# QK-normed attention and a token/channel mixer on one core: attention one element ahead, weights converted in two staggered halves, key norms in the exp's scale, a compact reciprocal

## The chip, the core and the metric

One core of a Trainium2 chip runs the whole program. The metric is the device time of one execution in microseconds. The kernel before takes 1813.64 us (median of 3 runs, 1812.88 to 1815.33).

## The reference

Eight elements, twelve heads, 448 tokens, 64 columns a head. The four mixer weights come in as 64-bit floats, everything else as 32-bit.

```python
def rmsnorm(x, g):
    return x / np.sqrt(np.mean(x * x, axis=-1, keepdims=True) + 1e-06) * g
scores = np.matmul(rmsnorm(q, g_q), rmsnorm(k, g_k).transpose(0, 1, 3, 2)) / np.sqrt(64)
attn = np.exp(scores - max(scores)); attn = attn / (sum(attn) + 1e-09)
x = (attn @ v), heads side by side              # (8, 448, 768)
h = np.maximum(x.transpose(0, 2, 1) @ w_tok1, 0.0) @ w_tok2      # 448 -> 256 -> 448
u = x + h.transpose(0, 2, 1)
return u + np.maximum(u @ w_ch1, 0.0) @ w_ch2                    # 768 -> 1536 -> 768
```

## The kernel before

**Two halves of the work.** Attention goes by pairs of heads: 8 elements x 6 pairs = 48 pairs, two steps each (`att_step`, L334). A step computes the scores of half of the key tokens (`score`, L242: four matmuls into four PSUM buffers of `ps_S`, then four exps on ScalarE into `e`), adds the exps of the key chunks on VectorE (`chunk_sums`, L286), and multiplies the exps of the step before with the values (`av`, L297). Once per pair a matmul with ones spreads the sums over the rows (`denominator`, L312), and VectorE takes the reciprocal (L328) and multiplies the products with it into `uT` (L329). The norms of the next pair (`norm_pair`, L202) are squares on GpSimd (L211), a sum on VectorE (L213), a power of -1/2 on GpSimd (L217) and the scaling of queries and keys on GpSimd (L221). `trans_qk` (L227) transposes them on TensorE into a buffer of `ps_M`, which has two, and copies them out with the gain, the queries on VectorE (L238) and the keys on ScalarE (L240). The mixing of an element (`mlp_items`, L449) transposes `uT` to `x` (L375), mixes tokens (L390, L398), then channels (L413 with `w_ch1`, L425 with `w_ch2`), transposes the result to `y` (L437) and stores it (L444). `x` and `y` share one buffer.

**Weights.** The 64-bit weights are split into 80 chunks of 256 columns: 4 of `w_tok1`, 4 of `w_tok2`, 36 of `w_ch1`, 36 of `w_ch2`. A chunk is loaded raw from ScalarE's queue (L137, buffers `raw`, three) and put together as a 32-bit float by `weight_convert` (L147): two masks (L162, L163), two steps for the exponent on GpSimd (L165, L166), one for the mantissa on ScalarE (L167), and three more on VectorE (L168, L170, L172). Chunk i's load is issued two chunks ahead.

**Order.** TensorE runs in the order in which the program writes its instructions. On the other engines and queues a planner orders the instructions by its own costs, and each engine then runs its list in order, DMA issues included. `merge` (L23) interleaves lists of items by their stated costs. First the 26 steps of elements 0 and 1 and two steps of element 2 are merged with the 44 chunks of `w_tok1`, `w_tok2` and `w_ch1` (L480). Then the mixing of each element b is merged with the attention of element b + 2 (`AHEAD`, L468). Beside the mixing of element 0, up to its last `w_ch1` matmul, lie the 36 chunks of `w_ch2` (L486). The last two elements mix alone. Ahead of all a comparison of the gains chooses between two copies of the body (L524); in this run the one with `shifted` False is taken.

## Time and profile before

| what | value |
|---|---|
| time, median of 3 runs | 1813.64 us |
| time of the profiled execution | 1814.12 us |
| its span, first to last instruction | 1811.9 us |
| mean granted TensorE clock (1 is 2.4 GHz, 0.5 is 1.2 GHz) | 0.941 |
| TensorE busy | 1570.2 us, 87% |
| VectorE busy | 627.2 us, 35% |
| GpSimd busy | 446.8 us, 25% |
| ScalarE busy | 355.1 us, 20% |
| DMA, mean over the span | 36 GB/s |

The shares are means over stages with different limits, so the stages are read apart: windows give the busy time of each engine, the granted clock and the DMA share of a stretch, and the waits of that stretch say what an idle engine was released by. "Idle before" in square brackets is the time that the engine did nothing ahead of an instruction, with what ended it.

### The profile page before, as it was taken

To read this page: it belongs to the slowest core of one execution; us is meant where nothing else is said; L and a number is where in the kernel's file an instruction comes from. 1 tells how busy PE (TensorE), PEld (TensorE's weight loads), DVE (VectorE), ACT (ScalarE), POOL (GpSimd) and SP (SyncE) were. 2 spreads that over 40 slices of the span, in tenths; PEclk is the share of its full clock that TensorE was granted. 3 is DMA by queue.
4 is the path that set the end of the run, shared out by engine and by line. 5 is a ranking of instruction groups with operands and counts; after the bars stand their busy time and mean duration, and the time that the engine had idled before them with its cause. 6 is when DMAs were issued, how large, how long until landed. Compare 5 with 4: busy or idle time off the path is not lost.

```text
span 1811.9 us, 13526 instructions
## 1 busy us (share of the span) xinstructions
PE 1570.2 (87%) x5248; PEld 743.7 (41%) x5248; DVE 627.2 (35%) x957; ACT 355.1 (20%) x713; POOL 446.8 (25%) x408
## 2 busy tenths in 40 slices
PE   4555456789989998999989998999989998998998
PEld 1121123334444444444444444444444444554554
DVE  4666667772224233322233233232332231000000
ACT  2222223232121211221121212221121211001100
POOL 5655555543111212112112212113113100000000
PEclk8776778989999999999999999999999999999999
DMA  3222223320100001000100001000100000000001
GB/s 97 77 82 75 76 67 95 97 73 26 36 31 16 31 16 46 29 18 16 46 31 16 31 16 56 21 16 28 33 31 16 11 1 31 0 0 31 1 0 32
DMA packets 53838, 65.73 MB, mean 36 GB/s; under 512 B 4164, under 2 KB 43844, under 8 KB 53764
## 3 DMA queue, kind: packets, MB, share of 16 engines
q1 hardware_dynamic: 41986, 44.05, 7.8%
q10 hardware_dynamic: 11778, 20.72, 3.7%
q8 instruction: 43, 0.70, 0.2%
q14 instruction: 31, 0.25, 0.0%
HBM read 53.74 MB, written 11.01 MB: 36 GB/s over the span
## 4 chain that ended last, share of the span: by engine, by line
PE 70%; DVE 13%; POOL 10%; DMA 2%; issue 2%; ACT 2%; ACTq 0%; DVEq 0%; POOLq 0%
PE m_ps L425 24%; PE m_ps L413 22%; PE s_ps L251 6%; PE o_ps L305 5%; PE m_ps L390 4%; DVE rd L328 4%; POOL rs L217 4%; PE m_ps L398 3%; DVE es L295 2%; POOL e_t L166 2%; POOL qs L221 2%; POOL e_t L165 2%; DMA out_dram<-y 2%; PE m_ps L375 2%; PE m_ps L233 1%
## 5 line engine op out<-in xcount | busy, mean ns | idle before, releaser
L413 PE MATMUL m_ps<-uT,wc_sb 128*128 128x448 f32 x1152 | 452.0, 547 | 13.3 <-ACT h L417 6.3
L425 PE MATMUL m_ps<-h,wc_sb 128*128 128x448 f32 x1152 | 450.4, 544 | 9.2 <-DVE uT L430 5.8
L413 PEld LDWEIGHTS m_ps<-uT,wc_sb 128*128 128x128 f32 x1152 | 215.9, 191 | 236.5 <-issue 209.6
L211 POOL TENSOR_TENSOR qs<-qk 112x512 f32<-112x512 f32 x96 | 102.4, 1068 | 830.4 <-PE m_ps L233 769.9
L425 PEld LDWEIGHTS m_ps<-h,wc_sb 128*128 128x128 f32 x1152 | 213.4, 190 | 220.3 <-issue 204.0
L256 ACT ACTIVATE e<-s_ps 112x448 f32<-112x448 f32 x384 | 180.9, 546 | 313.5 <-PE s_ps L251 211.1
L251 PE MATMUL s_ps<-qkT 64*112 64x448 f32 x768 | 191.3, 613 | 16.5 <-DVE qkT L238 6.5
L295 DVE TENSOR_TENSOR es<-es,e 112x896 f32<-112x896 f32 x96 | 108.1, 1126 | 213.8 <-ACT e L256 210.3
L233 PE MATMUL m_ps<-ident,qs 112*128 112x112 f32 x384 | 60.8, 287 | 138.2 <-DVE rd L328 105.2
L305 PE MATMUL o_ps<-e,vt 112*64 112x448 f32 x768 | 171.9, 571 | 0.0
L217 POOL TENSOR_TENSOR rs<-ms,mhalf_c 112x16 f32<-112x16 f32 x48 | 154.1, 3210 | 53.6 <-DVE ms L216 53.5
L430 DVE TENSOR_TENSOR uT<-uT,m_ps 128x448 f32<-128x448 f32 x48 | 29.8, 621 | 374.6 <-PE m_ps L425 374.6
L328 DVE RECIPROCAL rd<-m_ps 128x448 f32<-128x448 f32 x48 | 141.6, 2951 | 5.8 <-PE m_ps L319 5.8
L417 ACT ACTIVATE h<-m_ps 128x448 f32<-128x448 f32 x96 | 52.2, 543 | 403.0 <-PE m_ps L413 401.6
L233 PEld LDWEIGHTS m_ps<-ident,qs 112*128 112x128 f32 x384 | 46.3, 154 | 175.1 <-issue 138.6
L291 DVE TENSOR_TENSOR es<-e 112x896 f32<-112x896 f32 x48 | 52.7, 1099 | 187.3 <-ACT e L256 187.3
L251 PEld LDWEIGHTS s_ps<-qkT 64*112 64x112 f32 x768 | 67.8, 188 | 120.0 <-issue 89.6
L221 POOL TENSOR_TENSOR qs<-qk,rs 112x512 f32<-112x512 f32 x96 | 98.4, 1046 | 3.8
L305 PEld LDWEIGHTS o_ps<-e,vt 112*64 112x64 f32 x768 | 53.0, 143 | 111.4 <-issue 111.4
L390 PE MATMUL m_ps<-x,w_sb 112*128 112x384 f32 x256 | 93.7, 524 | 5.9 <-ACT h L393 5.9
L398 PE MATMUL m_ps<-w_sb,h 128*128 128x448 f32 x192 | 80.1, 559 | 13.7 <-DVE rd L328 11.1
L439 ACT COPY y<-m_ps 112x512 f32<-112x512 f32 x48 | 28.1, 586 | 293.1 <-PE m_ps L437 292.8
(40 smaller groups left out, 793.7 us busy)
## 6 DMA issues: line engine op xcount, KB each, us to landing
raw<-in_moe_w_ch_dram ACTq DMA_DIRECT2D x72, 256.0 KB, 2.6
qk<-in_q_dram SPq DMA_DIRECT2D x48, 224.0 KB, 2.7
qk<-in_k_dram SPq DMA_DIRECT2D x48, 224.0 KB, 2.9
vt<-in_v_dram SPq DMA_DIRECT2D x48, 224.0 KB, 3.0
out_dram<-y SPq DMA_DIRECT2D x16, 672.0 KB, 4.3
raw<-in_moe_w_tok_dram ACTq DMA_DIRECT2D x4, 224.0 KB, 5.1
raw<-in_moe_w_tok_dram ACTq DMA_DIRECT2D x2, 256.0 KB, 2.6
raw<-in_moe_w_tok_dram ACTq DMA_DIRECT2D x2, 192.0 KB, 2.3
```

Of the source, the lines that this page charges most:

```text
L217: nc.gpsimd.tensor_tensor(out=rs[0:R], in0=ms[0:R], in1=mhalf_c[0:R].to_broadcast([R, 2 * n]), op=ALU.pow)
L221: nc.gpsimd.tensor_tensor(out=st["qs", p, i][0:R].rearrange("p c h d -> p h c d"), in0=qk[0:R, i].rearrange("p h (c d) -> p h c d", d=D), ...
L233: nc.tensor.transpose(ps[:, c * R:(c + 1) * R], qs[0:R, c].rearrange("p h d -> p (h d)"), ident[0:R, 0:R])
L251: nc.tensor.matmul(out=ps[0:R, 0:S], lhsT=qkT[a * D:(a + 1) * D, 1, kc * R:(kc + 1) * R], rhs=qkT[a * D:(a + 1) * D, 0, :], start=True, st ...
L256: nc.scalar.activation(out=e[0:R, a, i, :], in_=pss[a][0:R, 0:S], func=AF.Exp)
L295: nc.vector.tensor_tensor(out=es[0:R], in0=es[0:R], in1=e[0:R, :, i, :], op=ALU.add)
L305: nc.tensor.matmul(out=o[a * D:(a + 1) * D, 0:S], lhsT=vt[0:R, a, kc * D:(kc + 1) * D], rhs=e[0:R, a, i, :], start=(kc == 0), stop=(kc == ...
L328: nc.vector.reciprocal(out=rd[:], in_=ps[:, 0:S])
L390: nc.tensor.matmul(out=ps[:, 0:HC], lhsT=w1_sb[0:R, c, jc * P:(jc + 1) * P], rhs=st["x"][0:R, c, cs], start=(c == 0), stop=(c == NS - 1))
L398: nc.tensor.matmul(out=ps[:, 0:S], lhsT=st["h1", jc][:, cc * P:(cc + 1) * P], rhs=w2_sb[:, jc].rearrange("p c r -> p (c r)"), start=(jc == ...
L413: nc.tensor.matmul(out=ps[:, 0:S], lhsT=wc1_sb[:, cc, f * P:(f + 1) * P], rhs=st["uT", b][:, cc, :], start=(cc == 0), stop=(cc == NC - 1))
L425: nc.tensor.matmul(out=ps[:, 0:S], lhsT=wc2_sb[:, f, cc * P:(cc + 1) * P], rhs=st["h2"][:, f, :], start=(f == 0), stop=(f == NF - 1))
```

## The change

Attention now runs one element ahead: element 0's attention alone, then the mixing of element b beside the attention of b + 1, and only the last element mixes alone. Before the first mixing 15 chunks of weights are converted; the other 65, and the last half of the chunk before them, are merged with the mixing of element 0 up to its fourth output column. A chunk is converted in two parts: the masks, exponent and mantissa steps of chunk i are written ahead of the last steps of chunk i - 1; the last multiplication goes from VectorE to GpSimd. Raw loads go out from SyncE's queue, the stores of the result from ScalarE's.

Squares are taken on ScalarE, for queries and keys at once, two pairs ahead; loads of queries and keys lie three pairs ahead, with heads side by side already in SBUF. Only the queries are scaled by their norms; those of the keys are the scale of the exp, which is read per row. Both copies of the transposed queries and keys are on ScalarE. The first of the three sums of exps goes to GpSimd. The denominators come half a pair earlier, and their reciprocal is taken in 14 columns: a transpose in blocks of 32 puts one copy of the sums in few columns, and a second transpose spreads the reciprocals over the rows. The first two loads and the first norms stand ahead of the branch.

```diff
-def whole(ctx, tc, shifted, q, k, v, ...):
+def whole(ctx, tc, shifted, pre, q, k, v, ...):
...
-    raw_pool = pool("raw_pool", 3)
-    cv_pool = pool("cv_pool", 2)
-    qk_pool = pool("qk_pool", 2)
+    raw_pool = pool("raw_pool", 4)
+    cv_pool = pool("cv_pool", 3)
     v_pool = pool("v_pool", 2)
-    qs_pool = pool("qs_pool", 2)
-    st_pool = pool("st_pool", 3)
     qkT_pool = pool("qkT_pool", 2)
     e_pool = pool("e_pool", 2)
-    es_pool = pool("es_pool", 2)
-    rd_pool = pool("rd_pool", 1)
-    uT_pool = pool("uT_pool", 3)
+    es_pool = pool("es_pool", 1)
+    rd_pool = pool("rd_pool", 2)
+    uT_pool = pool("uT_pool", 2)
...
+                second.append((P, moe_w_ch1[t * P:(t + 1) * P, o:o + n], wc1_sb[:, t, o:o + n], None))
         for o in range(0, C, WCOLS):
             for f in range(NF):
                 n = min(WCOLS, C - o)
-                second.append((P, moe_w_ch2[f * P:(f + 1) * P, o:o + n], wc2_sb[:, f, o:o + n], None))
-        return first, second
+                third.append((P, moe_w_ch2[f * P:(f + 1) * P, o:o + n], wc2_sb[:, f, o:o + n], None))
+        return first, second, third
...
     def weight_load(i):
...
-            nc.scalar.dma_start(
+            nc.sync.dma_start(
                 out=t[0:rows, 0:n, :].rearrange("p n w -> p (n w)"), in_=src.bitcast(U32))
...
+    def convert_first(i):
+        rows, src, dst, split = chunks[i]
+        n = src.shape[-1]
+        if src.dtype != I64:
+            return
+        hi = st["raw", i][0:rows, 0:n, 1]
+        e_t = cv_pool.tile([P, WCOLS], U32, name="e_t")
+        m_t = cv_pool.tile([P, WCOLS], U32, name="m_t")
+        st["cv", i] = e_t, m_t
+        e, m = e_t[0:rows, 0:n], m_t[0:rows, 0:n]
+        ef, mf = e.bitcast(F32), m.bitcast(F32)
+        nc.vector.tensor_scalar(e, hi, 0x7FF00000, None, ALU.bitwise_and)
+        nc.vector.tensor_scalar(m, hi, 0x000FFFFF, None, ALU.bitwise_and)
+        nc.gpsimd.tensor_scalar(ef, e, 1151.0 * 2**20, 896.0 * 2**20, ALU.min, ALU.max)
+        nc.gpsimd.tensor_scalar(e, ef, -896.0 * 2**20, 8.0, ALU.add, ALU.mult)
+        nc.scalar.activation(out=mf, in_=m, func=AF.Identity, bias=one_c[0:rows, 0:1], scale=2.0**-20)
...
+    def convert_last(i):
...
         nc.vector.scalar_tensor_tensor(
             out=mf, in0=lo, scalar=2.0**-52, in1=mf, op0=ALU.mult, op1=ALU.add)
         nc.vector.scalar_tensor_tensor(
             out=e, in0=hi, scalar=0x80000000, in1=e, op0=ALU.bitwise_and, op1=ALU.bitwise_or)
-        nc.vector.tensor_tensor(out=dst, in0=fold(mf), in1=fold(ef), op=ALU.mult)
+        nc.gpsimd.tensor_tensor(out=dst, in0=fold(mf), in1=fold(ef), op=ALU.mult)
...
             if i + LOADS_AHEAD < len(chunks):
                 weight_load(i + LOADS_AHEAD)
-            weight_convert(i)
+            if i < len(chunks):
+                convert_first(i)
+            if i:
+                convert_last(i - 1)
         return [(1.0, lambda i=i: one(i)) for i in range(lo, hi)]
...
+    def scale(p):
+        n = 2 * NS
+        for i in range(1 + shifted):
+            x = st["qk", p][0:R, i].rearrange("p c h d -> p (c h) d")
+            r = st["rs", p][0:R, i * n:(i + 1) * n]
+            nc.gpsimd.tensor_tensor(
+                out=x, in0=x, in1=r.unsqueeze(2).to_broadcast([R, n, D]), op=ALU.mult)
...
     def trans_qk(p, i):
...
             nc.tensor.transpose(
-                ps[:, c * R:(c + 1) * R],
-                qs[0:R, c].rearrange("p h d -> p (h d)"), ident[0:R, 0:R])
-        dst = st["qkT", p][:, i, :]
-        if i == 0:
-            nc.vector.tensor_scalar(dst, ps[:, 0:S], g_t[:, i:i + 1], None, ALU.mult)
-        else:
-            nc.scalar.mul(dst, ps[:, 0:S], g_t[:, i:i + 1])
+                ps[:, c * R:(c + 1) * R], qk[0:R, i, c].rearrange("p h d -> p (h d)"), ident[0:R, 0:R])
+        nc.scalar.mul(st["qkT", p][:, i, :], ps[:, 0:S], g_t[:, i:i + 1])
...
-                nc.scalar.activation(out=e[0:R, a, i, :], in_=pss[a][0:R, 0:S], func=AF.Exp)
+                r = 2 * NS + kc * 2 + a
+                nc.scalar.activation(
+                    out=e[0:R, a, i, :], in_=pss[a][0:R, 0:S], func=AF.Exp,
+                    scale=st["rs", p][0:R, r:r + 1])
...
-            nc.vector.tensor_tensor(out=es[0:R], in0=e[0:R, :, 0, :], in1=e[0:R, :, 1, :], op=ALU.add)
+            nc.gpsimd.tensor_tensor(out=es[0:R], in0=e[0:R, :, 0, :], in1=e[0:R, :, 1, :], op=ALU.add)
...
+        nb = S // 32
+        dt = rd_pool.tile([P, S], F32, name="dt", tag="rd")
+        if shifted:
+            nc.vector.tensor_scalar(dt[:], ps[:, 0:S], 1e-9, None, ALU.add)
+            src = dt[:]
+        else:
+            src = ps[:, 0:S]
+        nc.vector.transpose(out=dt[:], in_=src)
+        rc = pre.st_pool.tile([P, nb], F32, name="rc")
+        nc.vector.reciprocal(out=rc[:], in_=dt[:].rearrange("p (n c) -> p n c", c=32)[:, :, 0])
         rd = rd_pool.tile([P, S], F32, name="rd", tag="rd")
-        if shifted:
-            nc.vector.tensor_scalar(rd[:], ps[:, 0:S], 1e-9, None, ALU.add)
-            nc.vector.reciprocal(out=rd[:], in_=rd[:])
-        else:
-            nc.vector.reciprocal(out=rd[:], in_=ps[:, 0:S])
+        nc.vector.transpose(
+            out=rd[:].rearrange("p (n c) -> p n c", c=32), in_=rc[:].unsqueeze(2).to_broadcast([P, nb, 32]))
...
-        if g < NG and h == 0 and p + 2 < NP:
-            items.append((0.0, lambda: load_qk(p + 2)))
+        if g < NG and h == 0 and p + 3 < NP:
+            items.append((0.0, lambda: pre.load_qk(p + 3, st)))
...
         def products():
-            if h == 1 and p >= 1:
-                denominator(p - 1)
             if 1 <= g <= NG:
                 av(*divmod(g - 1, 2))
+            if h == 0 and p >= 1:
+                denominator(p - 1)
         def tiled():
             for part in (products, scores) if shifted else (scores, products):
                 part()
-        items.append((3.6 + 0.8 * h, tiled))
-        if g < NG and p + 1 < NP:
-            if h == 0:
-                items.append((0.0, lambda: norm_pair(p + 1)))
-            else:
-                items += [(0.4, lambda i=i: trans_qk(p + 1, i)) for i in range(2)]
+        items.append((4.4 - 0.8 * h, tiled))
+        if g < NG and h == 0 and p + 2 < NP:
+            items.append((0.0, lambda: pre.norm_pair(p + 2, st)))
+            items.append((0.0, lambda: scale(p + 2)))
+        if g < NG and h == 1 and p + 1 < NP:
+            items += [(0.4, lambda i=i: trans_qk(p + 1, i)) for i in range(2)]
...
-            nc.sync.dma_start(
+            nc.scalar.dma_start(
                 out=out[b].rearrange("(p c) n -> p c n", c=NS)[:, :, cs], in_=st["y"][0:R, :, cs])
...
-        early = items
-        late = []
+        early, late = items, []
         for cc in range(NC):
+            if cc == NC - WCOLS // P:
+                early, late = early + late, []
...
-    first, second = weight_chunks()
-    chunks = first + second
-    AHEAD = 2
-    load_qk(0)
+    first, second, third = weight_chunks()
+    chunks = first + second + third
+    AHEAD = 1
+    BEFORE = len(first) + NC + 1
     load_v(0)
-    load_qk(1)
     for i in range(LOADS_AHEAD):
         weight_load(i)
-    norm_pair(0)
+    scale(0)
     trans_qk(0, 0)
     trans_qk(0, 1)
+    pre.load_qk(2, st)
+    pre.norm_pair(1, st)
+    scale(1)
     per = NPAIR * 2
     att_items = lambda lo, hi: [it for g in range(lo, hi) for it in att_step(g)]
-    for _, fn in merge(att_items(0, AHEAD * per + 2), weight_items(0, len(first))):
+    for _, fn in merge(att_items(0, AHEAD * per + 2), weight_items(0, BEFORE)):
         fn()
     for b in range(B):
         early, late = mlp_items(b)
         if b == 0:
-            early = merge(early, weight_items(len(first), len(chunks)))
+            early = merge(early, weight_items(BEFORE, len(chunks) + 1))
...
+class Start:
+    def __init__(self, ctx, tc, q, k):
+        self.qk_pool = pool("qk_pool", 3)
+        self.sq_pool = pool("sq_pool", 1)
+        self.load_qk(0, self.st)
+        self.load_qk(1, self.st)
+        self.mhalf_c = const.tile([P, 1], F32, name="mhalf_c")
+        nc.gpsimd.memset(self.mhalf_c[:], -0.5)
+        self.norm_pair(0, self.st, apart=True)
+        self.ident = const.tile([P, P], F32, name="ident")
+        make_identity(nc, self.ident[:, :])
+        self.one_c = const.tile([P, D], F32, name="one_c")
+        nc.gpsimd.memset(self.one_c[:], 1.0)
+    def heads(self, p):
+        b, j = divmod(p, self.NPAIR)
+        return b, slice(2 * j, 2 * j + 2)
+    def load_qk(self, p, st):
+        b, hs = self.heads(p)
+        st["qk", p] = qk = self.qk_pool.tile([128, 2, self.NS, 2, self.D], F32, name="qk")
+        for i, src in enumerate((self.q, self.k)):
+            for a in range(2):
+                self.nc.sync.dma_start(
+                    out=qk[0:self.R, i, :, a], in_=src[b, hs][a].rearrange("(p c) d -> p c d", c=self.NS))
+    def norm_pair(self, p, st, apart=False):
+        nc, R, D = self.nc, self.R, self.D
+        n = 2 * self.NS
+        qk = st["qk", p]
+        sq = self.sq_pool.tile([128, 2, n, D], F32, name="sq")
+        ms = self.st_pool.tile([128, 2 * n], F32, name="ms")
+        st["rs", p] = rs = self.st_pool.tile([128, 2 * n], F32, name="rs")
+        for lo, hi in ((0, 1), (1, 2)) if apart else ((0, 2),):
+            nc.scalar.activation(
+                out=sq[0:R, lo:hi].rearrange("p i n d -> p (i n d)"),
+                in_=qk[0:R, lo:hi].rearrange("p i c h d -> p (i c h d)"), func=AF.Square)
+            nc.vector.tensor_reduce(
+                out=ms[0:R, lo * n:hi * n], in_=sq[0:R, lo:hi].rearrange("p i n d -> p (i n) d"),
+                axis=AX_X, op=ALU.add)
+            w = slice(lo * n, hi * n)
+            nc.vector.tensor_scalar(ms[0:R, w], ms[0:R, w], 1.0 / D, 1e-6, ALU.mult, ALU.add)
+            nc.gpsimd.tensor_tensor(
+                out=rs[0:R, w], in0=ms[0:R, w],
+                in1=self.mhalf_c[0:R].to_broadcast([R, (hi - lo) * n]), op=ALU.pow)
...
+    pre = Start(ctx, tc, q, k)
```

## Rows read from the trace of the kernel before

**Rows 1.** Timeline, PE: first transposes to x (L375). Start us, us, instruction.
```profile
290.21 3.50 PE L375 MATMUL m_ps<-ident,uT 128*112 128x128 f32 x16
...
518.53 1.32 PE L375 MATMUL m_ps<-ident,uT 128*112 128x128 f32 x8
...
1518.35 0.60 PE L375 MATMUL m_ps<-ident,uT 128*112 128x128 f32 x4
...
1661.40 0.60 PE L375 MATMUL m_ps<-ident,uT 128*112 128x128 f32 x4
```

**Rows 2.** Windows: length, busy PE, PEld, DVE, ACT, POOL; clock, DMA, GB/s.
```profile
23.30:290.20 266.90, 145.95 (x560) 55.47 (x561) 173.15 (x333) 75.50 (x160) 158.51 (x154) 0.74 0.24 76
290.20:518.50 228.30, 199.41 (x658) 93.37 (x656) 121.20 (x241) 54.85 (x112) 82.31 (x97) 0.95 0.20 58
...
719.00:919.50 200.50, 190.37 (x655) 90.44 (x655) 63.07 (x69) 39.21 (x79) 41.64 (x31) 0.98 0.09 28
1518.35:1661.40 143.05, 137.03 (x395) 71.89 (x393) 9.54 (x15) 13.77 (x25) 0.00 (x0) 0.98 0.03 10
```

**Rows 3.** Waits, 40 to 290 us: total us, times, longest.
```profile
PE m_ps L233 <- DVE rd L328: 105.2, 12, 11.5
...
ACT e L256 <- DVE m_t L168: 58.0, 10, 6.8
```

**Rows 4.** Timeline of ScalarE and its queue (ACTq) around 115 us.
```profile
115.01 0.33 ACTq L137 DMA_DIRECT2D raw<-in_moe_w_ch_dram  x1
115.39 0.54 ACT L256 ACTIVATE e<-s_ps 112x448 f32<-112x448 f32 x1 [5.69 <-DVE m_t L168]
```

**Rows 5.** Timeline of the start.
```profile
3.68 0.36 SPq L193 DMA_DIRECT2D qk<-in_q_dram  x1
...
6.28 1.04 POOL L211 TENSOR_TENSOR qs<-qk 112x512 f32<-112x512 f32 x1 [1.90 <-DMA qk<-in_q_dram]
...
11.88 1.28 ACT L167 ACT_TABLE_LOAD   x1 [11.88 <-DVE m_t L163]
...
23.29 3.33 PE L251 MATMUL s_ps<-qkT 64*112 64x448 f32 x8 [0.72 <-ACT qkT L240]
```

**Rows 6.** Groups, whole run: busy us, mean ns; the power by ns min/median/max.
```profile
L328 DVE RECIPROCAL rd<-m_ps 128x448 f32<-128x448 f32 x48 | 141.6, 2951 | 5.8 <-PE m_ps L319 5.8
L295 DVE TENSOR_TENSOR es<-es,e 112x896 f32<-112x896 f32 x96 | 108.1, 1126 | 213.8 <-ACT e L256 210.3
L211 POOL TENSOR_TENSOR qs<-qk 112x512 f32<-112x512 f32 x96 | 102.4, 1068 | 830.4 <-PE m_ps L233 769.9 <-issue 50.2 <-POOL qs L211 6.5
L417 ACT ACTIVATE h<-m_ps 128x448 f32<-128x448 f32 x96 | 52.2, 543 | 403.0 <-PE m_ps L413 401.6 <-DVE m_t L168 1.4
L240 ACT ACTIVATE qkT<-m_ps,g_t 128x448 f32<-128x448 f32 x48 | 30.4, 634 | 240.0 <-PE m_ps L233 238.1 <-DVE qkT L238 1.7
L217 POOL TENSOR_TENSOR rs<-ms,mhalf_c x48: 2893/2894/4492, 16.4 to 1431.9; 112x16 f32<-112x16 f32 x48
```

**Rows 7.** 290.2 to 400: e_t (DVE, POOL), raw (DVE), group L172, all engines.
```profile
290.20:400.00 109.80, 35.56 (x100) 37.08 (x66) 0.89 0.32 96
290.20:400.00 109.80, 48.35 (x133) 0.89 0.32 96
L172 DVE TENSOR_TENSOR wc_sb<-m_t,e_t 128x256 f32<-128x256 f32 x34 | 14.8, 437 | 0.0
290.20:400.00 109.80, 85.25 (x270) 40.08 (x270) 82.42 (x199) 32.38 (x68) 59.41 (x80) 0.89 0.32 96
```

**Rows 8.** Waits of PE, 290 to 518.5: total us, times, longest.
```profile
PE m_ps L390 <- ACT h L393: 5.9, 1, 5.9
...
PE m_ps L233 <- DVE qkT L238: 4.1, 2, 3.3
PE m_ps L398 <- DVE rd L328: 4.1, 1, 4.1
PE m_ps L413 <- DVE rd L328: 4.1, 3, 2.3
```

More of the change, by code (lines that the diff above doesn't have):

```diff
@@ L109, in weight_chunks @@
     def weight_chunks():
-        first, second = [], []
+        first, second, third = [], [], []
         w1v = moe_w_tok1.rearrange("(p c) n -> p c n", c=NS)
@@ L409, in ch1 @@
             st["m"] = m_tile()
+        assert st["ready"] >= len(first) + NC * (f * P // WCOLS + 1)
         ps = st["m"]
@@ L421, in ch2 @@
             st["m"] = m_tile()
+        assert st["ready"] >= len(first) + len(second) + NF * (cc * P // WCOLS + 1)
         ps = st["m"]
```

84 lines of the change are left out of this document (30 added, 54 removed).

## The prediction

> **What bounds the kernel now.** I read the windows first, cut where the first transposes of an element's mixing stand on TensorE. The first lie at 290.21, those of element 1 at 518.53, of element 6 at 1518.35, of the last at 1661.40 [rows 1]. So the profiled span of 1811.9 us is: 290.2 of attention alone (elements 0 and 1) beside 44 weight chunks; 228.3 for element 0's mixing with element 2's attention and the other 36 chunks; five periods of (1518.35 - 518.53) / 5 = 200.0; 143.05 for element 6 without attention; 150.5 for the last and its store. Two kinds of time stand there. In a period TensorE is busy 190.4 of 200.5 at a clock of 0.98 (nearly all at the higher level), in the element without attention 137.0 of 143.05 [rows 2]: bound by TensorE, and nothing but its work counts. From 23.3 to 290.2 it is busy 146 of 267 at a clock of 0.74, VectorE 173, GpSimd 159, ScalarE 76 [rows 2]: nobody is full, so it is a chain.
>
> The waits name the chain. The twelve transposes of queries and keys wait 105.2 us, 8.8 each, for the reciprocal of the denominators, which holds a PSUM buffer that they need; and ten exps wait 58 us for a weight instruction on VectorE [rows 3]. Why an exp should wait for that is seen in the timeline: a raw weight load is issued from ScalarE's queue at 115.01 and the exp starts at 115.39 after 5.69 us of idling [rows 4]. The load waits until VectorE has read the raw buffer it will overwrite, and what is queued behind it on ScalarE, the exps, waits with it. A step (two per pair of heads, 26 in all) takes (290.2 - 23.3) / 26 = 10.27 us, where its TensorE work is 146 / 26 = 5.6 at that clock, and (190.4 - 137.0) / 12 = 4.45 in a period [rows 2].
>
> **The change, part by part.** *One element ahead.* Element 0's attention alone is 14 steps in place of 26, and one more element mixes with attention beside it. The span becomes start + 14 steps + batch 0 + 6 x 200.0 + 150.5, against start + 26 steps + 228.3 + 5 x 200.0 + 143.05 + 150.5. At unchanged paces this is 12 x 10.27 - (200.0 - 143.05) = 66 us less, if batch 0 can carry 66 chunks (65 and a half, counted as 66) in place of 36.
>
> *Start.* Queries and keys are loaded and normed ahead of the branch. Now the first load goes out at 3.68, is read at 6.28 (2.6 later), and the first score stands at 23.29 [rows 5]. I add: four loads from about 1.1 on, some 0.4 apart, the last landing near 5.3; square about 1, sum and scale 0.9, power at least 2.89 [rows 6], scaling 1.07 [rows 6], transposes 1.9, copy 0.63 [rows 6]; 13.7, and 0.8 for hand-overs: 14.5. The square, the sum and the transposes are estimates from the 512-wide passes near them. Queries and keys now land in pieces of a quarter of the size. Landing could stay 2.6 or grow fourfold to 10; hidden three pairs ahead later, it is open here only: 12 to 22. I take the lower half because the queues are empty at that time.
>
> *A step of the head.* Three waits go. Raw loads move to SyncE's queue, so no exp stands behind them: 58 us over the 24 steps from 40 to 290 [rows 3], 2.4 a step. The reciprocal of 2.95 [rows 6] becomes two transposes and a reciprocal of 14 columns. No row has a transpose; the bounds are 0.6 each, a VectorE pass of the like size without a division (an estimate: 0.43 per 256 columns [rows 7] gives 0.7 for 448), and 2.95, the slowest pass there is. I take 0.6, because nothing in it iterates; the short reciprocal is 14/448 of 2.95 and an overhead, 0.25. The norms are two pairs ahead with three buffers, so the transposes no longer wait for GpSimd. What comes next is TensorE's own order: 5.6 of work a step at the clock of 0.74, plus once per pair the two copies of 0.63 on ScalarE (both there now) between the last transpose and the next score, 1.27 a pair, 0.63 a step. Sum 6.25. It is below that (4.45 + 0.45 = 4.9) if the clock rises. Other engines, per step: GpSimd has the power (2.89 to 4.49, say 3.7), one scaling, and the moved sum of 896 columns (1.07 x 896/512 = 1.87), halved 3.3, and 15/14 chunks of 1.12 + 0.55, 1.8: 5.1. ScalarE has 8 exps whose scale is now read per row (0.54 [rows 4], and 0.09 more, the difference of copy and Relu at the same shape [rows 6]), two copies and the square (0.543 x 1024/448 = 1.24 at most), halved 3.8. Neither passes 6.25. So 14 x 6.25 = 87.5, and batch 0 begins at 102.
>
> *Batch 0.* TensorE's floor is the period, 200. The 66 chunks all lie in the part up to the fourth output column, by the items' costs 113 of 133, 171 us. VectorE: the reads of raw cost 48.35 / 33 = 1.47 a chunk and the multiply 0.44 [rows 7]. Its busy time of 121.2 [rows 2] less 33 x 1.91 is 58.2; less 6 x (2.95 + 1.13 + 0.63), the reciprocal, one sum and one copy [rows 6], and with 6 x 1.45 back, 38.6; with 66 x 1.47, 136. GpSimd: 82.3 less 33 x 1.12 is 45.3; less 13 squares and 6 key scalings at 1.07, 25; with 6 x 1.87, 36; with 66 x (1.12 + 0.55), 146. The 0.55 for the moved multiply is half of the 512-wide multiply on GpSimd [rows 6]; the other end, by the power's own spread on this engine (4.49 / 2.89 = 1.55 while VectorE is busy), is 0.85. Both engines fit in 171 at 0.80 to 0.85 busy, a little over what VectorE reaches here now (82.4 of 109.8 over the first part, 0.75 [rows 7]). SyncE's queue now holds the raw loads behind four loads per pair and the value loads. In exchange the store's issue goes to ScalarE behind the copy that it waits for, and the exps stand behind it for one issue only. If a value load blocks SyncE, a chunk comes late; there are about ten chunks of lead at the first wide matmuls, three at the second, so I price it at nothing there and at up to 8 us at the second.
> TensorE's own stalls in this stage now are waits for Relus on ScalarE, the longest 5.9, and 4.1 + 4.1 + 4.1 on the reciprocal and a copy by VectorE [rows 8]. The first kind is the queue of the raw loads again and goes; the second I keep, since VectorE is as full as before: 200 + 12 = 212.
>
> *The periods.* TensorE's work is unchanged. Each loses the waits on the long reciprocal and gains GpSimd's sum between the exps and the denominators: half a step of room, at a GpSimd that is busy 42 of 200 [rows 2]. I price both at nothing; without that cover a denominator would wait under 2 us per pair, 12 a period. The store before x is reused stays. 6 x 200.0 + 150.5 = 1350.5.
>
> **Sum.** 102 + 212 + 1350.5 = 1664.5, and 2.2 between span and time (1814.1 against 1811.9): **1667 us**. The profiled execution took 0.5 more than the median, which is nothing here. The likeliest case itself reaches from 1648 to 1688.
>
> **Rivals.** *GpSimd sets the pace.* For it: its instructions stretch while VectorE reads two operands, the power by 1.55 [rows 6], and it takes over two kinds of work. Against it: 1.12 a chunk was measured under just such load. With a stretch of 1.35 to 1.5 on everything, a head step is about 7.1 and batch 0 some 240: 14.5 + 100 + 240 + 1350.5 + 2.2 = 1707 (1688 to 1720). The same comes if the two transposes are nearer 2.95. The Trainium skill, GPSIMD Engine Reference, "Elementwise — side-by-side cycle accounting", puts a two-input pass at 1.96 of VectorE's time; by that the moved multiply is an estimated 0.86, 20 us more in batch 0 and some 1690 in all; no row of this run shows that multiply on GpSimd.
> *The head's pace stays* (the change doesn't do what it says): something else holds 10.27 a step. 14.5 + 144 + 212 + 1350.5 + 2.2 = 1723. Against it: 8.8 and 4.8 us of each pair's 20.5 are two named waits whose cause is edited away.
> *TensorE all through.* Steps of 4.9, batch 0 at 200, periods at 198: 83 + 200 + 1188 + 150.5 + 2.2 = 1624 (to 1648). For it: in the mixed stages the clock is near 1 as soon as TensorE is fed.
> *The square needs another table.* ScalarE loads a table once, 1.28 us [rows 5], for exp, Relu and copies. If the square is not in it, each pair loads two: 2.6 us, 18 in the head and up to 15 in batch 0, hidden elsewhere: about 1690. The Trainium skill, ScalarE: Activation LUTs, "Table sets: the hidden batching unit", says cheap functions are in every set as filler, but does not name the square among them; nothing in this trace uses it.
> *Slower: the conversion holds batch 0.* All 66 chunks now stand between TensorE and its weights. In the head of the kernel before a chunk took 267 / 44 = 6.07 us; at that pace batch 0 is 66 x 6.07 + 30 = 431, and the time 14.5 + 87.5 + 431 + 1350.5 + 2.2 = 1886. It decides from (1811.9 - 1350.5 - 102 - 30) / 66 = 5.0 us a chunk. Against it: 33 chunks took 109.8 us here, 3.3 each, with the longer VectorE share [rows 7].
>
> **How the numbers follow.** The forecast has 0.52, GpSimd's pace 0.20, TensorE all through 0.13, the head's pace kept 0.08, the table 0.04, conversion 0.03. The range 1625 to 1716 takes in the forecast, nearly all of the second and third, and the table: 0.84. Faster by over 0.2% (about what can be told from no change here) 0.96, within it 0.01, slower 0.03.
>
> **What would show it.** Right: the mixing's first transposes near 102 and 314, then every 200 us; exps without waits on VectorE's weight work; no wait of transposes on denominators; GpSimd about 0.75 busy in batch 0. Wrong: wide matmuls waiting for the converted weights, GpSimd over 0.9 in batch 0, table loads beside squares, a period over 202, or a first score after 22.

## The result, and the profile after

The changed kernel takes **1735.05 us** (median, 1733.93 to 1737.66) against 1814.43 before, a ratio of 0.9565 (95% interval 0.9549 to 0.9582). The forecast was 1667, in a range of 1625 to 1716: the direction was right, but 79 us came in place of 147. The profiled execution has a span of 1734.2.

*Where the 68 us are.* The timeline of TensorE in the changed kernel, first transposes of an element's mixing (now L367); they answer [rows 1]:

```profile
140.38 3.29 PE L367 MATMUL m_ps<-ident,uT 128*112 128x128 f32 x16
...
386.20 1.14 PE L367 MATMUL m_ps<-ident,uT 128*112 128x128 f32 x8 [0.24 <-ACT y L433]
...
1584.50 0.60 PE L367 MATMUL m_ps<-ident,uT 128*112 128x128 f32 x4
```

| stretch | forecast | measured |
|---|---|---|
| start, to the first score | 14.5 | 15.27 |
| head, 14 steps | 87.5 (6.25 a step) | 125.1 (8.94 a step) |
| batch 0 | 212 | 245.8 |
| six periods | 1200 | 1198.3 (199.7 each) |
| last element | 150.5 | 149.7 |

Start, periods and end are right; the head misses by 38, batch 0 by 34. In the windows of the changed kernel (columns as in [rows 2]), batch 0 is cut in two where the last weight chunk but three has been begun:

```profile
15.30:140.40 125.10, 81.25 (x297) 31.20 (x297) 87.33 (x177) 59.32 (x108) 104.27 (x115) 0.76 0.34 97
140.40:257.00 116.60, 72.55 (x224) 34.47 (x225) 97.08 (x200) 39.91 (x78) 99.93 (x138) 0.81 0.40 111
257.00:386.20 129.20, 126.49 (x434) 59.13 (x432) 33.87 (x52) 35.42 (x62) 30.83 (x24) 1.00 0.12 30
386.20:586.50 200.30, 190.18 (x657) 90.66 (x657) 43.50 (x63) 53.26 (x91) 35.93 (x18) 0.98 0.11 28
```

The second half of batch 0 runs as a period does, TensorE 126.5 of 129.2 at full clock. The whole loss of batch 0 lies in its first 117 us, where TensorE is busy 72.6 at a clock of 0.81 while VectorE (0.83) and GpSimd (0.86) work through 43 chunks. Of all 80 chunks, 34 begin in the head and three after 257: the planner placed them well ahead of the code's order, by which, as in my sum, 15 lie in the head and the rest over 171 us.

*What TensorE waits for.* The waits of TensorE in the head (15.3 to 140.4), then in batch 0 (140.4 to 386.2); they answer [rows 3] and [rows 8]:

```profile
PE m_ps L216 <- POOL qk L207: 27.9, 5, 8.3
PE s_ps L231 <- ACT qkT L218: 11.6, 7, 5.4
PE s_ps L231 <- ACT e L237: 4.9, 2, 2.5
...
PE m_ps L406 <- ACT h L410: 16.0, 2, 15.8
PE m_ps L390 <- DVE uT L395: 10.3, 3, 6.8
PE m_ps L382 <- DVE dt L314: 9.5, 1, 9.5
PE m_ps L406 <- DVE dt L314: 7.7, 1, 7.7
```

The 105.2 of [rows 3] are gone. In the head TensorE works 81.25 / 14 = 5.8 a step (5.6 in the sum), and stands 44.4 us in these three lines, 3.2 a step where I had 0.63. In batch 0 the four lines are 43.5 where I had 12. Together these seven lines are 88 us where the sum had 21: the difference, 67, is about the miss. It is not exact: the sum's 200 for batch 0 already held the 10 us that TensorE idles in a period, and TensorE's own work took 199.0 there, 9 more than in a period, at a clock of 0.91 (the two halves of batch 0 above). These two nearly cancel.

*The queue of ScalarE* ahead of the 15.8, in the timeline:

```profile
239.77 0.51 ACT L156 ACTIVATE m_t<-m_t,one_c 128x256 f32<-128x256 uint32 x1 [2.38 <-DVE m_t L152]
...
251.07 0.51 ACT L156 ACTIVATE m_t<-m_t,one_c 128x256 f32<-128x256 uint32 x1 [4.07 <-DVE m_t L152]
251.49 0.52 ACT L410 ACTIVATE h<-m_ps 128x448 f32<-128x448 f32 x1
252.07 4.27 PE L406 MATMUL m_ps<-uT,wc_sb 128*128 128x448 f32 x6 [15.79 <-ACT h L410]
```

TensorE's product was finished near 236. The Relu (L410) that frees its PSUM buffer stands behind conversion passes (L156) that wait for VectorE's mask; so ScalarE idles with the Relu ready. *The queue of VectorE* ahead of the 9.5 shows the same with GpSimd:

```profile
151.52 0.92 PE L302 MATMUL m_ps<-es,one_c 112*64 112x448 f32 x4
...
154.72 0.43 DVE L174 SCALAR_TENSOR_TENSOR e_t<-raw,e_t 128x256 uint32<-128x256 uint32 x1 [2.94 <-POOL e_t L155]
156.76 0.29 DVE L151 TENSOR_SCALAR e_t<-raw 128x256 uint32<-128x256 uint32 x1 [1.61 <-POOL wc_sb L176]
...
160.10 0.43 DVE L174 SCALAR_TENSOR_TENSOR e_t<-raw,e_t 128x256 uint32<-128x256 uint32 x1 [1.59 <-POOL e_t L155]
...
164.01 0.64 DVE L314 STREAM_TRANSPOSE dt<-m_ps 128x448 f32<-128x448 f32 x1
```

The sums that L314 reads (L302) were done at 152.4; the transpose starts at 164.0, and VectorE idled three times in between.

*One buffer for queries and keys.* The timeline from the transposes of pair 3 to those of pair 4:

```profile
69.48 1.75 PE L216 MATMUL m_ps<-ident,qk 112*128 112x112 f32 x8 [8.26 <-POOL qk L207]
71.31 1.23 SPq L524 DMA_DIRECT2D qk<-in_q_dram  x2
76.59 1.06 ACT L536 ACTIVATE sq<-qk 112x1024 f32<-112x1024 f32 x1
77.68 1.22 DVE L539 TENSOR_REDUCE ms<-sq 112x16 f32<-112x1024 f32 x1
81.95 2.91 POOL L544 TENSOR_TENSOR rs<-ms,mhalf_c 112x16 f32<-112x16 f32 x1
84.93 2.45 POOL L207 TENSOR_TENSOR qk<-qk,rs 112x512 f32<-112x512 f32 x1
87.44 1.76 PE L216 MATMUL m_ps<-ident,qk 112*128 112x112 f32 x8 [4.98 <-POOL qk L207]
```

Nothing is three pairs ahead: the next load goes out when the last pair has been transposed, and load, square, sum, power, scaling and transposes follow one another, 18 us a pair. In the built program the tiles of pairs 0 and 1, taken in `Start` ahead of the branch, keep their two addresses to themselves, and all later pairs lie at the third address.

*Prices.* Groups of the whole run, which answer [rows 6]:

```profile
L314 DVE STREAM_TRANSPOSE dt<-m_ps 128x448 f32<-128x448 f32 x48 | 31.1, 648 | 134.6 <-PE m_ps L302 134.6
L316 DVE RECIPROCAL rc<-dt 128x14 f32<-128x14 f32 x48 | 11.5, 240 | 1.4
L237 ACT ACTIVATE e<-s_ps,rs 112x448 f32<-112x448 f32 x384 | 213.5, 633 | 177.7 <-PE s_ps L231 174.5 <-POOL e_t L154 3.2
L274 POOL TENSOR_TENSOR es<-e 112x896 f32<-112x896 f32 x48 | 100.2, 2087 | 73.9 <-PE m_ps L302 73.3
L176 POOL TENSOR_TENSOR wc_sb<-m_t,e_t 128x256 f32<-128x256 f32 x72 | 61.8, 860 | 15.7 <-DVE e_t L174 10.5 <-DVE m_t L172 1.4
L536 ACT ACT_TABLE_LOAD x1 | 1.3, 1283 | 5.1 <-DMA qk<-in_q_dram 5.1
```

### The profile page after: what moved, and what is told of

It is laid out like the page before. It is cut to its first block, busy times and chain, and to the rows that moved or that the text cites. A ratio compares the mean times of both kernels' runs of the same rounds, so it can differ in the third digit from the quotient of the medians.

```text
span 1734.2 us, 13947 instructions
## 1 busy us (share of the span) xinstructions
PE 1558.9 (90%) x5248; PEld 740.4 (43%) x5248; DVE 490.7 (28%) x831; ACT 465.0 (27%) x810; POOL 447.6 (26%) x393
## 4 chain that ended last, share of the span: by engine, by line
PE 79%; POOL 6%; DVE 6%; DMA 3%; ACT 2%; issue 2%; SPq 1%; ACTq 0%; DVEq 0%; POOLq 0%
PE m_ps L419 26%; PE m_ps L406 25%; PE s_ps L231 8%; PE o_ps L288 8%; PE m_ps L382 5%; PE m_ps L390 4%; DMA qk<-in_k_dram 2%; PE m_ps L302 2%; PE m_ps L216 2%; POOL rs L544 1%; POOL wc_sb L176 1%; SPq L524 1%; POOL e_t L154 1%; DMA raw<-in_moe_w_ch_dram 1%; DVE uT L424 1%
## 5 line engine op out<-in xcount | busy, mean ns | idle before, releaser
L544 POOL TENSOR_TENSOR rs<-ms,mhalf_c 112x16 f32<-112x16 f32 (+1 forms) x49 | 140.4, 2866 | 981.2 <-DVE ms L543 980.6
L237 ACT ACTIVATE e<-s_ps,rs 112x448 f32<-112x448 f32 x384 | 213.5, 633 | 177.7 <-PE s_ps L231 174.5
L231 PE MATMUL s_ps<-qkT 64*112 64x448 f32 x768 | 184.1, 594 | 16.5 <-ACT qkT L218 11.6
L539 DVE TENSOR_REDUCE ms<-sq 112x16 f32<-112x1024 f32 (+1 forms) x49 | 58.5, 1196 | 293.2 <-ACT sq L536 293.2
L410 ACT ACTIVATE h<-m_ps 128x448 f32<-128x448 f32 x96 | 51.9, 541 | 308.0 <-PE m_ps L406 308.0
L218 ACT ACTIVATE qkT<-m_ps,g_t 128x448 f32<-128x448 f32 x96 | 60.6, 633 | 221.7 <-PE m_ps L216 217.9
L274 POOL TENSOR_TENSOR es<-e 112x896 f32<-112x896 f32 x48 | 100.2, 2087 | 73.9 <-PE m_ps L302 73.3
L216 PE MATMUL m_ps<-ident,qk 112*128 112x112 f32 x384 | 57.1, 278 | 49.5 <-POOL qk L207 40.7
L288 PEld LDWEIGHTS o_ps<-e,vt 112*64 112x64 f32 x768 | 47.9, 140 | 116.0 <-issue 114.7
L536 ACT ACTIVATE sq<-qk 112x1024 f32<-112x1024 f32 (+1 forms) x49 | 50.7, 1037 | 119.7 <-DMA qk<-in_k_dram 118.5
L216 PEld LDWEIGHTS m_ps<-ident,qk 112*128 112x128 f32 x384 | 46.3, 150 | 84.8 <-issue 38.9
```

Source lines behind the costliest of these rows:

```text
L216: nc.tensor.transpose(ps[:, c * R:(c + 1) * R], qk[0:R, i, c].rearrange("p h d -> p (h d)"), ident[0:R, 0:R])
L218: nc.scalar.mul(st["qkT", p][:, i, :], ps[:, 0:S], g_t[:, i:i + 1])
L231: nc.tensor.matmul(out=ps[0:R, 0:S], lhsT=qkT[a * D:(a + 1) * D, 1, kc * R:(kc + 1) * R], rhs=qkT[a * D:(a + 1) * D, 0, :], start=True, st ...
L237: nc.scalar.activation(out=e[0:R, a, i, :], in_=pss[a][0:R, 0:S], func=AF.Exp, scale=st["rs", p][0:R, r:r + 1])
L274: nc.gpsimd.tensor_tensor(out=es[0:R], in0=e[0:R, :, 0, :], in1=e[0:R, :, 1, :], op=ALU.add)
L288: nc.tensor.matmul(out=o[a * D:(a + 1) * D, 0:S], lhsT=vt[0:R, a, kc * D:(kc + 1) * D], rhs=e[0:R, a, i, :], start=(kc == 0), stop=(kc == ...
```

## The experiments

After the result there were three theories. **A**, one buffer: the pair's chain sets the head. **B**, GpSimd's pace, above all the multiply that it took over. **C**, the planner: conversions are placed so early that passes which release TensorE stand behind them on in-order engines. All runs are compared with the kernel before, which took 1814 to 1818 in each group of runs, so that differences between runs of two groups are good to some 4 us; where `Start` is inside the branch all line numbers behind it are one higher, and the first score stands at 18 in place of 15. The last column but two is the time from the end of batch 0 to the end of the profiled span: six periods and the last element, without any chunk.

| run | mixing starts | batch 0 | behind it | median | ratio to before (95%) |
|---|---|---|---|---|---|
| changed kernel | 140.4 | 245.8 | 1348.0 | 1735.05 | 0.9565 |
| e1 start inside the branch | 128.3 | 259.2 | 1347.0 | 1737.24 | 0.9566 (0.9548 to 0.9584) |
| e2 multiply on VectorE | 131.1 | 232.7 | 1349.7 | 1714.67 | 0.9436 (0.9420 to 0.9453) |
| e3 e1 + e2 | 119.1 | 239.0 | 1345.4 | 1705.46 | 0.9389 (0.9371 to 0.9407) |
| e4 e1 + written order on all engines | 124.7 | 235.4 | 1338.1 | 1699.33 | 0.9353 (0.9336 to 0.9370) |
| e5 e4 + e2 | 124.9 | 239.2 | 1336.6 | 1702.06 | 0.9361 (0.9345 to 0.9377) |
| e6 e5 + first sum on VectorE | 128.8 | 245.9 | 1338.0 | 1715.41 | 0.9443 (0.9428 to 0.9459) |
| e7 conversion of one pass | 123.0 | 194.9 | 1348.3 | 1668.82 | 0.9180 (0.9165 to 0.9196) |
| e8 e1 + e7 | 87.5 | 204.2 | 1347.2 | 1642.59 | 0.9042 (0.9027 to 0.9058) |
| e9 e1 + ScalarE in written order | 106.5 | 252.9 | 1334.7 | 1695.94 | 0.9332 (0.9313 to 0.9351) |
| e10 e1 + SyncE in written order | 103.7 | 269.1 | 1347.0 | 1721.72 | 0.9472 (0.9454 to 0.9490) |
| e11 e1 + ScalarE's pass on VectorE | 128.7 | 257.7 | 1344.4 | 1735.14 | 0.9550 (0.9532 to 0.9569) |
| e12 e4 + ScalarE's pass on VectorE | 92.0 | 235.0 | 1336.3 | **1664.76** | **0.9158** (0.9142 to 0.9175) |
| e13 e1 + VectorE in written order | 98.2 | 247.5 | 1337.7 | 1684.48 | 0.9277 (0.9255 to 0.9300) |
| e14 e12 + e2 | 94.6 | 236.3 | 1337.8 | 1670.48 | 0.9196 (0.9173 to 0.9218) |
| e15 e12, 12 more chunks in the head | 118.2 | 216.2 | 1336.0 | 1673.99 | 0.9221 (0.9201 to 0.9242) |
| e16 e13 + ScalarE's pass on VectorE | 99.4 | 230.8 | 1336.5 | 1667.59 | 0.9182 (0.9162 to 0.9203) |

**e1: three buffers that rotate.** `Start` is made inside the branch, so that its buffers come free there.

```diff
-def whole(ctx, tc, shifted, pre, q, ...
+def whole(ctx, tc, shifted, q, ...
     ctx.enter_context(tc.manual_schedule(engines={nc.tensor.engine}))
+    pre = Start(ctx, tc, q, k)
...
-    pre = Start(ctx, tc, q, k)
```

> The first two loads and the first norms stand inside the chosen copy of the body instead of ahead of the branch; all else as in the changed kernel. In the changed kernel every pair from the third on is loaded into one and the same buffer, because the buffers of the first two pairs stay taken until the branch ends; inside, the three buffers rotate. Theory A (one buffer): each pair of the head runs load, square, sum, power, scaling, transposes one after another, 17.9 us; with three buffers a step falls from 8.94 to 6.3 to 7.2 us, the first score comes some 3 us later, the mixing begins near 112 in place of 140, batch 0 stays at 246 or grows by up to 15 because fewer chunks are converted ahead: 1705 to 1720 us. Theory B (GpSimd sets the pace, 104 of 125 us busy in the head): steps stay near 8.9 and the time is 1735 to 1740 us.

The head ends 12 us earlier, batch 0 is 13 longer, the sum the same. The wait of the transposes for the scaling is gone, and the work that the planner puts beside the head fills its place: GpSimd is busy 104.4 of 113.0 us there (15.3 to 128.3).

**e2 and e3: the multiply back on VectorE,** with one buffer and with three.

```diff
-        nc.gpsimd.tensor_tensor(out=dst, in0=fold(mf), in1=fold(ef), op=ALU.mult)
+        nc.vector.tensor_tensor(out=dst, in0=fold(mf), in1=fold(ef), op=ALU.mult)
```

> The last multiplication of a weight chunk is on VectorE again, as before the change; all else as in the changed kernel. It took 28 us of GpSimd in the head and 41 in the first mixing. Theory B (GpSimd sets the pace): the head falls by up to 28 us and the first mixing by up to 30: 1680 to 1710 us. Theory A (one buffer in the head, and the planner's early conversions in the first mixing): the head stays within 5 us, the first mixing within 10, since VectorE takes up the same work at half the time each: 1722 to 1740 us.

> Both edits: the start inside the branch and the last multiplication on VectorE. Theory A: about the time of the start inside alone, within 10 us, 1700 to 1720. Theory B: about the time of the multiplication on VectorE alone, 1680 to 1710. If both limits lie close behind each other, the two together gain more than either, 1670 to 1695.

This one line is worth 20 us, and 32 where the buffers rotate. e2 lies between what A and B let expect and e3 in both ranges; that the gain grows where the buffers rotate speaks for B.

**e4: the written order on every engine,** in e1's kernel: the planner places nothing.

```diff
-    ctx.enter_context(tc.manual_schedule(engines={nc.tensor.engine}))
+    ctx.enter_context(tc.manual_schedule(engines={nc.tensor.engine, nc.vector.engine, nc.scalar.engine, nc.gpsimd.engine, nc.sync.engine}))
```

> The start inside the branch, and all engines and SyncE's queue issue their instructions in the order in which the program writes them, not only TensorE. In the changed kernel the planner puts 33 of the 80 chunks into the head, where the program writes 15, and the other 47 into the first 117 us of the first mixing, where Relus and sums that TensorE waits for stand behind them in the queues. Theory C (the planner's early conversions cost the first mixing its 46 us over a period): written in order, 15 chunks fall in the head and the others spread over 170 us; the first mixing falls from 246 to 205 to 220 and the head to about 105: 1660 to 1690 us. Theory B: the first mixing stays near 240, as GpSimd has the same work in it or more: 1705 to 1730. If the written order itself leaves engines waiting for each other in every element, the periods grow over 200 us and the time with them.

38 us less than e1 with the same instructions, so C holds a good part, though less than the 1660 to 1690 expected. Of the 38, 27 lie in the head and batch 0 and 9 behind them, where nothing is converted: with VectorE or ScalarE in the written order the stretch behind batch 0 takes 9 to 12 us less, in this run and in those below; the reason stays open. 15 chunks begin in the head and 65 in batch 0. What is left in the head is one line of TensorE's waits:

```profile
PE s_ps L232 <- ACT qkT L219: 30.3, 7, 6.1
```

The copies of queries and keys stand on ScalarE behind conversion passes now by the code's own order.

**e5 and e6: GpSimd's two added passes back on VectorE, in the written order.** e5 has e2's line; e6 besides

```diff
-            nc.gpsimd.tensor_tensor(out=es[0:R], in0=e[0:R, :, 0, :], in1=e[0:R, :, 1, :], op=ALU.add)
+            nc.vector.tensor_tensor(out=es[0:R], in0=e[0:R, :, 0, :], in1=e[0:R, :, 1, :], op=ALU.add)
```

> As the run with the start inside the branch and every engine in the written order (1699), with the last multiply of each weight chunk back on VectorE. GpSimd's pace: the same edit took 32 us off where three query-key buffers rotate (1737 to 1705), so 1699 - 25 to 32 = 1667 to 1675, the head's mixing starting near 110 and batch 0 near 220. If in the written order the head is held by TensorE's own order and ScalarE's copies (it waited 30 us for them), VectorE gets fuller without a gain: 1690 to 1700.

> As the run before, and the first sum of exps (896 columns) back on VectorE too, so that both passes that the change moved to GpSimd are undone. GpSimd's pace still: 13 sums of 2.1 us leave GpSimd in the head and in batch 0, another 10 to 20 us: 1655 to 1665, less in batch 0 than in the head. VectorE next: its busy share is already the higher one with the multiply, so the sum costs what it frees: equal to the run before or up to 10 us slower (1675 to 1685).

In the written order the same line that gave 32 us gives nothing (1699.3 to 1702.1), though GpSimd is busy 108 of the 235 us from 120 to 355, where in e4 it is busy 170 of batch 0's 235. Theory B fails as a cause by itself: in the planner's order GpSimd's pace costs time, in the written order it doesn't. That it counts where VectorE's queue waits for GpSimd ahead of something that TensorE needs fits both, but no run shows it alone. The sum on VectorE costs 13 us: there the change was right.

**e7 and e8: what the conversion costs at all,** with one buffer and with three. A chunk is converted by one VectorE pass, which takes the high word alone.

```diff
@@ convert_first, from the line behind its return
-        hi = st["raw", i][0:rows, 0:n, 1]
...
-        nc.scalar.activation(out=mf, in_=m, func=AF.Identity, bias=one_c[0:rows, 0:1], scale=2.0**-20)
@@ convert_last
         t = st.pop(("raw", i))
-        e_t, m_t = st.pop(("cv", i))
...
-        nc.gpsimd.tensor_tensor(out=dst, in0=fold(mf), in1=fold(ef), op=ALU.mult)
+        nc.vector.tensor_scalar(dst, fold(t[0:rows, 0:n, 1]), 2.0**-32, None, ALU.mult)
```

> The changed kernel with the weights' conversion cut to one VectorE pass per chunk (the values are then not the reference's; loads, chunks and their places stay). Of about 2.8 us of GpSimd's and 2.2 us of VectorE's work per chunk, 0.5 on VectorE stay. GpSimd's pace: the head goes down to the 6.25 us a step of the forecast or below (mixing at 90 to 105), batch 0 to 200 to 210, 1640 to 1665. One buffer for queries and keys: the chain of a pair (load 1.9, square, sum, power, scaling, transposes) stays near 15 us, so the mixing starts at 115 to 130 although GpSimd is idle, batch 0 at 205: 1665 to 1690.

> The same cut of the conversion with the start inside the branch (three rotating query-key buffers). The difference to the run before is the price of the one buffer once GpSimd and VectorE are out of the way: 15 to 30 us if the pair's chain is the second limit, which gives 1640 to 1660 and a mixing at 90 to 100; nothing if the chain was never a limit by itself.

The windows of the head and of batch 0, e7 and then e8:

```profile
15.30:123.00 107.70, 75.91 (x297) 29.96 (x297) 56.12 (x107) 45.52 (x75) 47.13 (x21) 0.78 0.58 172
123.00:317.90 194.90, 189.90 (x657) 90.11 (x656) 50.85 (x84) 53.59 (x92) 36.20 (x18) 0.99 0.19 54
```

```profile
15.30:87.50 72.20, 62.68 (x304) 25.16 (x304) 45.74 (x95) 47.13 (x79) 53.63 (x25) 1.00 0.80 228
87.50:291.70 204.20, 192.78 (x658) 91.46 (x657) 57.51 (x102) 53.64 (x92) 40.67 (x20) 0.97 0.23 67
```

Without the conversion batch 0 is 51 us shorter and as long as a period: all of its loss is the conversion's, and 17 of the head are. What is left of the head is the one buffer: e8 takes 35 us off it and 26 off the time. TensorE's own time in the head falls with it, from 75.9 at a clock of 0.78 to 62.7 at 1.00. So A is real, 26 us, but hidden while the planner fills the head with chunks (e1). With the first score at 18.2, the head's floor is (87.5 - 18.2) / 14 = 4.95 a step.

**e9, e10 and e13: one more engine in the written order,** each in e1's kernel.

```diff
-    ctx.enter_context(tc.manual_schedule(engines={nc.tensor.engine}))
+    ctx.enter_context(tc.manual_schedule(engines={nc.tensor.engine, nc.scalar.engine}))
```

(`nc.sync.engine` in e10, `nc.vector.engine` in e13.)

> The start inside the branch, and ScalarE's instructions (with TensorE's, as before) in the written order; the planner still places VectorE, GpSimd and SyncE. If the loss of batch 0 is TensorE waiting for Relus and copies that the planner put behind conversions on ScalarE, most of the 36 us of the run with every engine in the written order comes already here: 1700 to 1712, no wait for a Relu over 6 us. If it is how early the chunks are converted, the time stays within 8 us of the run with the start inside (1737).

> The start inside the branch, and SyncE's transfers in the written order: a chunk's raw load can't be issued ahead of its turn among the query, key and value loads, so that conversions can't run ahead; ScalarE, VectorE and GpSimd stay with the planner. If it is how early the chunks are converted: head at 14 to 20 chunks, mixing from 105 to 115, batch 0 spread over its length, 1700 to 1715. If it is the places on ScalarE's queue: 1725 to 1740.

> The start inside the branch, VectorE (with TensorE) in the written order, ScalarE, GpSimd and SyncE placed by the planner. ScalarE's order alone gave 1696 of 1737. If the passes that release TensorE stood behind conversions on ScalarE only, this gives little: 1725 to 1740. If VectorE's order holds the conversions back as well, so that ScalarE's pass is never early: 1700 to 1715.

The waits of TensorE in batch 0 for the Relus and for the transposes of the denominators (in e1 16 and 15 us), of e9 and then of e13, where none for those transposes is above 1 us:

```profile
PE m_ps L407 <- DVE dt L315: 15.2, 2, 8.7
...
PE m_ps L407 <- ACT h L411: 0.5, 2, 0.2
```

```profile
PE m_ps L407 <- ACT h L411: 14.3, 2, 10.3
```

ScalarE's order alone gives 41 us, about as much as all five together, and VectorE's alone 53. Of these, 12 and 9 lie behind batch 0, so the head and batch 0 get 28 and 42 us shorter. Holding back the loads alone (e10) gives 16: the head ends 25 us earlier and batch 0 is 10 longer, and TensorE still waits in it for Relus (25 us) and residual sums (12). e9, e10 and e13 all begin 14 to 17 chunks in the head, where e1 begins 28. So how early the chunks are taken is worth some 15 us, by which e10's batch 0 ends sooner; the other 13 of e9 and 27 of e13 come from what stands behind the chunks: each order takes away most of the waits for its own engine. For e13 I had expected at most 37 us; VectorE is the first engine of a chunk's chain, and with it in order ScalarE's and GpSimd's passes can't be early either.

**e11, e12 and e16: ScalarE's conversion pass on VectorE,** with the planner, in the written order, and with VectorE alone in order.

```diff
-        nc.scalar.activation(out=mf, in_=m, func=AF.Identity, bias=one_c[0:rows, 0:1], scale=2.0**-20)
+        nc.vector.tensor_scalar(mf, m, 2.0**-20, 1.0, ALU.mult, ALU.add)
```

> The start inside the branch, and the one conversion pass that stands on ScalarE (mantissa scaled and biased) on VectorE, 80 passes of some 0.3 to 0.45: ScalarE then holds exps, copies, Relus and squares alone, and a chunk goes over two engines instead of three. If TensorE's waits come from ScalarE's queue: 1705 to 1720 although VectorE gets 30 us more. If GpSimd's pace alone counts: 1737 within 6, since its work is the same. If VectorE is the next limit: 1745 to 1760.

> The same pass moved to VectorE with every engine in the written order (1699 with the pass on ScalarE). There TensorE waits 30 us in the head and 23 us in batch 0 for ScalarE's copies and Relus, which stand behind that pass: 1665 to 1685 if these waits go. If VectorE, busy 146 of 235 in batch 0 and then 175, stretches in its turn: 1700 to 1715.

> The start inside, the scaling pass on VectorE and VectorE in the written order; ScalarE holds no conversion, GpSimd and SyncE stay with the planner. With the planner placing VectorE this edit gave 1735, with every engine written 1665. If what matters is that no pass that releases TensorE stands behind conversions on its queue: 1665 to 1680. If the places on GpSimd or SyncE matter too: 1695 to 1720.

The waits of TensorE, of e11 in batch 0, then of e12 in the head and in batch 0:

```profile
PE m_ps L407 <- DVE dt L315: 32.1, 2, 26.6
```

```profile
PE m_ps L303 <- DVE es L279: 6.8, 5, 2.6
PE s_ps L232 <- ACT qkT L219: 5.9, 7, 0.9
...
PE m_ps L432 <- DVE uT L425: 12.9, 2, 12.6
PE m_ps L407 <- DVE dt L315: 5.6, 2, 4.6
```

e11 shows it most sharply: the waits for ScalarE's Relus vanish, and a wait of 26.6 us for one transpose of denominators comes in their place, since the planner puts that transpose behind conversions on VectorE. The time is the same; I had put that time down to GpSimd's pace, but the waits name VectorE's queue. With the order kept the same edit is worth 35 us: e12, **1664.76 us**, 0.9158 of the kernel before, beats both kernels. With VectorE alone in order (e16) it is worth 17.

**e14 and e15: is anything left in the balance?** e14 has e2's line in e12's kernel; e15 has

```diff
-    BEFORE = len(first) + NC + 1
+    BEFORE = len(first) + NC + 1 + 12
```

> As the best run (1665: start inside, every engine in the written order, the scaling pass on VectorE), with the last multiply back on VectorE as well. If GpSimd's pace still costs anything once the queues are in order: 1645 to 1660 (GpSimd stood 0.87 busy from 165 to 255 us). If VectorE, 0.88 busy there, is the equal limit, 66 x 0.44 = 29 us more on it cost up to that: 1670 to 1690.

> As the best run (1665), with 27 chunks in place of 15 beside the attention that runs alone, and 54 in place of 66 beside the first mixing. If both stretches are filled by GpSimd and VectorE alike, the sum of the two stays: 1660 to 1670. If the head has room (its step is 5.5 us) and batch 0 has none, 12 chunks less there are worth 12 x (235 - 200) / 66 = 6 us, less what the head gets: 1655 to 1665. If the head is the fuller one: 1670 to 1690.

The multiply costs 6 us on VectorE here, and the other split 9: head plus batch 0 end at 327.0 in e12, 330.9 in e14 and 334.4 in e15. e8 is there at 291.7, so the conversion still holds some 35 us in e12 (the times lie only 22 apart, since e12's periods are shorter, 11 us in all). VectorE (0.78) and GpSimd (0.75) are the busy engines of its batch 0. Which of the two bounds it was not separated.

## Why the prediction was right or wrong

**Right.** The overlap of one more element: six periods and a last element as forecast (1348.0 against 1350.5). The start (15.27 against 14.5). The transpose and the short reciprocal (0.65 and 0.24 against 0.6 and 0.25): the long wait of the transposes for the reciprocal is gone. The exps no longer stand behind raw loads. The row scale costs the exp 0.09, and there is one table load: the rival of the square's table did not happen. The periods hide GpSimd's new sum.

**Wrong: "The norms are two pairs ahead with three buffers, so the transposes no longer wait for GpSimd."** They wait 27.9 us for it, 4.6 to 8.3 in each of five pairs. I counted the pool's buffers and did not ask which of them were taken ahead of the branch. Priced by e8 against e7: 26 us, though it shows only when the conversion is out of the way.

**Wrong: "15/14 chunks" a step and 66 chunks over 171 us.** I read the list that the code merges; but only TensorE follows it. The planner took 34 chunks into the head and 43 into the next 117 us. The busy shares that I worked out (0.80 to 0.85) came near in those 117 us (0.83 and 0.86), and yet TensorE idled 44 us there.

**Wrong: "The first kind is the queue of the raw loads again and goes."** The wait for a Relu went from 5.9 [rows 8] to 15.8. Raw loads were one thing ahead of the exps and Relus on ScalarE; the conversion pass was another, it was in the trace of before, and it stayed. There the Relu (L393) of that wait stands behind raw loads (L137) and two such passes (L167):

```profile
305.69 0.51 ACT L167 ACTIVATE m_t<-m_t,one_c 128x256 f32<-128x256 uint32 x1 [2.46 <-DVE m_t L163]
307.74 0.33 ACTq L137 DMA_DIRECT2D raw<-in_moe_w_ch_dram  x1
308.69 0.51 ACT L167 ACTIVATE m_t<-m_t,one_c 128x256 f32<-128x256 uint32 x1 [2.49 <-DVE m_t L163]
309.10 0.47 ACT L393 ACTIVATE h<-m_ps 128x384 f32<-128x384 f32 x1
309.62 2.92 PE L390 MATMUL m_ps<-x,w_sb 112*128 112x384 f32 x4 [5.88 <-ACT h L393]
```

My 3.8 a step for ScalarE leaves this pass out altogether. My argument "both engines fit" was of the wrong kind: a chunk's chain goes VectorE, GpSimd and ScalarE, VectorE, GpSimd over in-order queues, and passes that release TensorE stand behind those of the chunks, also while an engine idles at a hand-over. The runs show it from three sides: take the conversion away (e7: batch 0 falls by 51, to a period), keep the instructions and put one engine in order (e9: 28 us off the head and batch 0, e13: 42), move a pass without the order (e11: the wait moves with it). More buffers for the conversion were not tried; from 15.3 to 257 VectorE waited 9 us for one to come free (L151 on L176) and 30 for GpSimd's exponent (L174 on L155).

**Terms mis-sized: the moved multiply,** 0.55 against 0.86 measured, the other end that I had given; back on VectorE it gives 20 us (e2), under the planner's order only. The Trainium skill, GPSIMD Engine Reference, "Elementwise — side-by-side cycle accounting", puts a two-input pass at 1.96 of VectorE's time; 0.86 against the 0.437 of [rows 7] is 1.97 (both means), so the trace agrees, and the value to take was that one. **VectorE's four passes on a chunk,** 1.47 in the sum, took 2.00 in the mean of the changed kernel, so that its busy share came near with a wrong term.

**The rivals.** GpSimd's pace gave 1707, with 7.1 a step for 8.94 and batch 0 at 240 for 245.8. It had a part in the changed kernel, the 20 us of e2, but is not the cause by itself: e5 and e14 take the multiply off GpSimd and gain nothing. The head's pace kept is nearest in time, 1723, by luck: its 10.27 a step is too long, and its batch 0 of 212 has none of the loss there. TensorE all through (1624 to 1648, steps of 4.9, batch 0 at 200) is what e8 shows, at 1643 with 4.95 and 204, with the conversion cut to one pass. That the queue order of two engines would hold TensorE was no rival of mine, though [rows 3] had shown one case of it. What stays open: how the miss splits between A and C in the changed kernel itself, since they overlap. The written order with `Start` ahead of the branch was not tried: by the code the load of pair p + 3 would then stand on SyncE ahead of the values of pair p + 1, and wait, with one buffer, for transposes that TensorE reaches only behind products of these values.
